# Layer five's VectorE order, and third-round sums and products two blocks at a time, in a DCN-v2 cross network on one core

## The chip, the cores and the metric

One core of one Trainium2 chip runs the whole kernel. The metric is the device time of one execution in microseconds, as a median over runs. Five engines work in parallel and wait for each other on semaphores: TensorE (PE in the profile, with PEld for its weight loads), VectorE (DVE), ScalarE (ACT), GpSimd (POOL) and SyncE (SP, which here issues nearly all DMAs; a queue's own instructions stand as SPq or ACTq).

## The reference

The inputs are `x0` (4096 x 416), six matrices `ws` (416 x 416 each) and six biases `bs`, all bfloat16.

```python
def reference(x0, ws, bs):
    x = x0
    for l in range(ws.shape[0]):
        x = x0 * (x @ ws[l] + bs[l]) + x
    return x
```

## The kernel before, in words

The layers are taken as x(l+1) = x0 * c(l+1), where c gathers 1 plus the sum of all products x @ w + b so far. Layers one to five work on transposed data (features on the 128 partitions, rows of the batch along the free dimension); the sixth layer turns back to rows, so that the result can be written out.

**Tiles.** The batch is cut in two halves of 2048 rows (`s` = 0, 1). The 416 features are three blocks of 128 (`m` = 0, 1, 2) and a remainder of 32, which is packed four groups to a tile. So a layer has six main tiles (s, m), called A, Bt, C (s = 0) and Dt, E, F (s = 1) in layer five, and two remainder tiles. Each main tile is evicted from PSUM in two pieces of 1024 columns (`h` = 0, 1).

**Layer five** is `feeding_layer`, and its VectorE work is written out by hand; `pin` keeps that order on the engine. For each tile ScalarE evicts a piece to a buffer `t` (L332). VectorE adds it to the running sum `CM` (`add`, L340, 128x1024), then multiplies by x0 into `XH`, the input of layer six (`mul`, L344, one 128x2048 operation for most tiles). When a tile's sum is complete and `mul` has read it, `rows_out` adds layer six's bias in place (L348) and SP issues a DMA transpose (`xl_dmat`, L231) that brings the sum to row order in `XLrows`, for the addition in layer six. `rem` and `rem_out` do the same for the remainder (L373, L375, L379), and `xl_rem` copies it on ScalarE to its place in `XLrows` (L311). SP works through its DMAs in the order of the program: the transposes of A, Bt, C, Dt, E and F, and after them all the outputs.

**Layer six** has four rounds of eight blocks of 128 rows. In a round TensorE makes eight products of 128x416 in four two-bank PSUM tiles. ScalarE casts a product from PSUM to a `t` buffer (L505). VectorE adds `XLrows` in place (the sum, L507), then multiplies by `X0rows` into an `o` buffer (the product, L495). SP then issues the output DMA (L496). `pending` delays each product until after the next sum, so that it doesn't stand right behind its own sum. In rounds one and two (layout `PAIRS`) two blocks that lie side by side in one PSUM tile are cast, summed, multiplied and written together. In round three (`TURNS`) the first two blocks go together and the other six singly. In round four (`ENDS`) all eight go singly; TensorE itself adds the row sums of the last three, and the very last block is multiplied straight from PSUM, its output issued by ScalarE's queue.

The buffers that turn over here are six `t` (`tpool`), ten `o` (`opool`) and four PSUM tiles.

Of the kernel before, what the change touches and what calls it, by code (L numbers as in the profile page):

```python
# [10 lines left out]
ALU = mybir.AluOpType  # L11
# [5 lines left out]
def kernel(  # L17
# [7 lines left out]
    nc = tc.nc  # L25
    B, D = x0.shape
# [19 lines left out]
    out_v = out.rearrange("(bt p) d -> p bt d", p=P)  # L46
# [11 lines left out]
    X0rows = big.tile([P, NBT, D], BF16)  # L58
# [11 lines left out]
    def col0(s, g):  # L70
        return SW * s + CW * g
# [8 lines left out]
    def pin(ins):  # L80
        tc.keep_in_program_order(ins)
# [33 lines left out]
    for g in range(1, NG):  # L115
        dst, src = WR[32 * g:32 * g + 32, 0, :], WR[0:R, 0, :]
# [113 lines left out]
    def xl_dmat(s, k):  # L230
        nc.sync.dma_start_transpose(out=XLrows[:, 16 * s:16 * s + 16, 128 * k:128 * k + 128],  # L231
                                    in_=CM[:, k, SW * s:SW * s + SW])
# [73 lines left out]
    def xl_rem(s):  # L306
        dst = XLrows[:, 16 * s:16 * s + 16, NK * P:D].rearrange("p (g i) r -> p i g r", g=NG)
        src = scrR[s][:].rearrange("p i (g r) -> p i g r", g=NG)
        n = 4 if s else 2
        for i in range(0, 4, n):  # L310
            pin(nc.scalar.copy(dst[:, i:i + n], src[:, i:i + n]))  # L311
# [13 lines left out]
    def feeding_layer(l, cur, curR, nxt, nxtR):  # L325
        tiles = [(s, m) for s in range(NS) for m in range(NK)]
        pts, ts = {}, {}

        def evict(t):
            for h in range(2):  # L330
                ts[t + (h,)] = tpool.tile([P, 2 * CW], BF16, name="t")
                nc.scalar.activation(ts[t + (h,)][:], pts[t][h][:].rearrange("p a b -> p (a b)"), ACT.Identity,  # L332
                                     bias=bM[:, t[1], l:l + 1], scale=1.0)

        def c_of(t, h):
            c0 = col0(t[0], 2 * h)
            return CM[:, t[1], c0:c0 + 2 * CW]

        def add(t, h):
            pin(nc.vector.tensor_tensor(out=c_of(t, h), in0=ts[t + (h,)][:], in1=c_of(t, h), op=ALU.add))  # L340

        def mul(t, h=0, n=2):
            c0, w = col0(t[0], 2 * h), n * CW
            pin(nc.vector.tensor_tensor(out=nxt[t[0]][:, t[1], 2 * CW * h:2 * CW * h + w], in0=CM[:, t[1], c0:c0 + w],  # L344
                                        in1=XM0[:, t[1], c0:c0 + w], op=ALU.mult))

        def last_bias(c, bias):
            pin(nc.vector.tensor_scalar(out=c, in0=c, scalar1=bias, scalar2=None, op0=ALU.add))  # L348

        def rows_out(t):  # L350
            s, m = t
            c = CM[:, m, SW * s:SW * s + SW]
            if s:
                c = c.rearrange("p (g r) -> p g r", g=NG)[:, :, 0:CW // 2]
            last_bias(c, bM[:, m, LL:L])
            xl_dmat(s, m)

        A, Bt, C, Dt, E, F = tiles
        layer_products(l, 0, tiles, pts, cur, curR, evict)
        evict(Bt)  # L360
        pr2 = psum.tile([P, 2, CW], FP32, tag="ps", name="pr2")
        for s in range(NS):
            mm_rem(l, s, pr2[:, s, :], cur, curR)
        tr = []
        for s in range(NS):
            tr.append(tpool.tile([P, 2 * CW], BF16, name="t"))
            for a in range(0, CW, CW // 2):
                nc.scalar.activation(tr[s][:, a:a + CW // 2], pr2[:, s, a:a + CW // 2], ACT.Identity, bias=bR[:, l:l + 1], scale=1.0)

        def rem(s, op):  # L370
            part = slice(CW * s, CW * s + CW)
            if op == ALU.add:
                pin(nc.vector.tensor_tensor(out=CR[:, part], in0=tr[s][:, 0:CW], in1=CR[:, part], op=op))  # L373
            else:
                pin(nc.vector.tensor_tensor(out=nxtR[:, part], in0=CR[:, part], in1=XR[0][:, part], op=op))  # L375

        def rem_out(s):
            last_bias(CR[:, CW * s:CW * s + (CW // 2 if s else CW)], bR[:, LL:L])
            nc.sync.dma_start_transpose(out=scrR[s][:], in_=CR[:, CW * s:CW * s + CW])  # L379

        add(A, 0)
        mul(A, 0)
        add(A, 1)
        add(Bt, 0)
        mul(A, 1)
        rows_out(A)
        add(Bt, 1)
        rem(0, ALU.add)
        mul(Bt, 0, 4)
        rem(0, ALU.mult)  # L390
        rem(1, ALU.add)
        rem_out(0)
        rows_out(Bt)
        rem(1, ALU.mult)

        layer_products(l, 2, tiles, pts, cur, curR, evict)
        evict(Dt)
        add(C, 0)
        add(C, 1)
        rem_out(1)  # L400
        mul(C, 0, 4)
        add(Dt, 0)
        rows_out(C)
        add(Dt, 1)
        mul(Dt, 0, 4)

        def before_last(t):
            xl_rem(0)
            evict(t)

        layer_products(l, 4, tiles, pts, cur, curR, before_last)
        evict(F)
        add(E, 0)
        rows_out(Dt)
        add(E, 1)
        mul(E, 0, 4)
        add(F, 0)
        rows_out(E)
        add(F, 1)
        mul(F, 0, 4)  # L420
        rows_out(F)
        xl_rem(1)

    cur, curR = XH[0:2], XR[1]
    for l in range(1, LL):
        nxt, nxtR = [[h for h in XH if h is not cur[0] and h is not cur[1]][0], cur[0]], XR[1 + (l % 2)]
        if l == LL - 1:
            feeding_layer(l, cur, curR, nxt, nxtR)
            cur, curR = nxt, nxtR
            break  # L430
        tiles = [(s, m) for s in range(NS) for m in range(NK)]
        pts = {}

        def finish(t):
            for h in range(2):
                ew_main(l, t[0], t[1], h, pts[t][h], nxt)

        for n in range(0, len(tiles), 2):
            layer_products(l, n, tiles, pts, cur, curR, finish)
            finish(tiles[n + 1])  # L440
            if n == 0:
                rem_pair(l, cur, curR, nxtR)
        cur, curR = nxt, nxtR

    l = LL
# [37 lines left out]
    pending = []  # L483

    def rows(q, g0, n):
        s, i = quads[q]
        b0 = 16 * s + 4 * g0 + i
        return slice(b0, b0 + 4 * (n - 1) + 1, 4)

    def close_product():  # L490
        while pending:
            src, q, g0, n, eng = pending.pop()
            b = rows(q, g0, n)
            o = opool.tile([P, 2, D], BF16, name="o")
            pin(nc.vector.tensor_tensor(out=o[:, 0:n, :], in0=src, in1=X0rows[:, b, :], op=ALU.mult))  # L495
            eng.dma_start(out_v[:, b, :], o[:, 0:n, :])  # L496

    def ew(q, g0, n, src, eng, added, direct):
        if direct:
            close_product()  # L500
            pending.append((src, q, g0, n, eng))
            return
        t = tpool.tile([P, 2 * CW], BF16, name="t")
        tv = t[:, 0:n * D].rearrange("p (a d) -> p a d", a=n)
        nc.scalar.copy(tv, src)  # L505
        if not added:
            pin(nc.vector.tensor_tensor(out=tv, in0=tv, in1=XLrows[:, rows(q, g0, n), :], op=ALU.add))  # L507
        close_product()
        pending.append((tv, q, g0, n, eng))

    PAIRS = [(0, 0), (0, 1), (1, 0), (1, 1), (2, 0), (2, 1), (3, 0), (3, 1)]
    TURNS = [(0, 0), (0, 1), (1, 0), (2, 0), (3, 0), (1, 1), (2, 1), (3, 1)]
    ENDS = [(0, 0), (1, 0), (2, 0), (0, 1), (3, 0), (1, 1), (2, 1), (3, 1)]
    rounds = [(0, PAIRS, 2), (2, PAIRS, 2), (4, TURNS, 2), (6, ENDS, 1)]
    for q, at, done in rounds:
        tiles = [psum.tile([P, 2, CW], FP32, tag="ps", name=f"py{n}") for n in range(4)]
        bank = [tiles[n][:, a, :] for n, a in at]

        final = q + 2 == NQ

        def close(u, n):
            tl, a = at[u]
            ew(q + u // 4, u % 4, n, tiles[tl][:, a:a + n, 0:D], nc.scalar if final and u == 7 else nc.sync,
               final and u >= 5, final and u == 7)

        for u in range(done):
            if q == 0:
                mm_q_open(q, u, bank[u])
            else:
                mm_q_full(q, u, bank[u], False)  # L530
        mm_q_rem(q, bank[0:4], done)
        close(0, done)
        mm_q_rem(q + 1, bank[4:8], 0)
        for u in range(done, 8):
            mm_q_full(q + u // 4, u % 4, bank[u], True, final and u >= 5)
            if at is not PAIRS:
                close(u, 1)
            elif u % 2:
                close(u - 1, 2)
    close_product()  # L540


# [28 lines left out]
```

## Time and profile before

| | us |
|---|---|
| median of 3 runs | 129.75 (129.72 to 129.80) |
| the profiled execution: its own time | 129.89 |
| the profiled execution: span in the trace | 128.1 |
| outside the span | 1.79 |
| PE busy | 122.5 (96% of the span) |
| DVE busy | 102.9 (80%) |
| ACT busy | 87.7 (68%) |

The granted TensorE clock of the profiled execution is 0.997 over the span. The span runs from the first instruction to the last; times below are in us from its start. In a timeline an instruction is given with its start, its duration, engine, line, operation, out<-in with sizes, and a count where neighbours are merged. VectorE's instructions overlap at their ends, so what one of them costs the next is read from start to start, and not from its duration.

### The profile page before, as it was taken

What the parts mean: (1) busy time and instruction counts of PE and PEld (TensorE: products, weight loads), DVE (VectorE), ACT (ScalarE), POOL (GpSimd) and SP (SyncE); (2) the same over time, 40 slices, a digit from 0 to 9 for tenths busy, and PEclk for the clock granted to TensorE, in tenths of its full rate; (3) what the DMA queues carried; (4) which work ended last, traced back from release to release, by engine and by line L of the source; (5) the groups of instructions that cost most, each with busy time, mean ns of one, the idle gap of its engine ahead of it and who ended that gap; (6) DMA issues with size and microseconds to landing.
All of it is one profiled execution on the core that took longest, in us unless ns stands there. A gap on an engine that the chain in (4) does not pass through costs nothing.

```text
span 128.1 us, 3968 instructions
## 1 busy us (share of the span) xinstructions
PE 122.5 (96%) x1684; PEld 55.3 (43%) x1686; DVE 102.9 (80%) x198; ACT 87.7 (68%) x109; POOL 5.6 (4%) x18
## 2 busy tenths in 40 slices
PE   7999999999999999999999999999999999999960
PEld 3343343444445444444444445444444345445530
DVE  0124579774979898989898989898999999999990
ACT  0038867887858667858667858667859697679740
POOL 4004002500000000000000000000000000000000
PEclk9999999999999999999999999999999999999998
DMA  3999999999950000000000000000089999999764
GB/s 99 232 229 223 178 235 263 304 331 335 339 155 0 5 0 0 8 0 5 0 5 0 5 0 5 0 0 5 0 164 91 176 168 213 157 303 292 248 199 142
DMA packets 42230, 16.38 MB, mean 128 GB/s; under 512 B 31034, under 2 KB 42212, under 8 KB 42212
## 3 DMA queue, kind: packets, MB, share of 16 engines
q1 hardware_dynamic: 37432, 15.40, 53.2%
q10 hardware_dynamic: 4780, 0.72, 3.6%
q8 instruction: 13, 0.21, 0.7%
q14 instruction: 5, 0.04, 0.1%
HBM read 6.15 MB, written 3.41 MB: 75 GB/s over the span
## 4 chain that ended last, share of the span: by engine, by line
PE 86%; DMA 4%; DVE 3%; ACTq 2%; issue 1%; ACT 0%; DVEq 0%
PE pt L208 50%; PE ph L240 11%; PE py L463 10%; PE pt L214 5%; PE pr L224 5%; DMA xrig<-in_x_dram 4%; DVE t L507 2%; PE pr L220 2%; PE ph L247 1%; PE py L476 1%; DVE o L495 1%; PE py L457 1%; ACTq L86 1%; ACTq L108 1%; ACT t L505 0%
## 5 line engine op out<-in xcount | busy, mean ns | idle before, releaser
L208 PE MATMUL pt<-XH,WM 128*32 128x512 bf16 x1152 | 65.2, 379 | 0.0
L187 ACT ACTIVATE t<-pt,bM 128x1024 bf16<-128x1024 f32 x36 | 37.2, 1115 | 13.7 <-PE pt L214 13.7
L208 PEld LDWEIGHTS <-WM 128*32 128x32 bf16 x1152 | 29.7, 97 | 33.8 <-issue 5.1
L188 DVE TENSOR_TENSOR CM<-t,CM 128x1024 bf16<-128x1024 bf16 x36 | 24.7, 687 | 4.3 <-ACT t L187 4.3
L189 DVE TENSOR_TENSOR XH<-CM,XM 128x1024 bf16<-128x1024 bf16 x36 | 24.9, 692 | 2.6
L505 ACT CAST t<-py 128x416 bf16<-128x416 f32 (+1 forms) x22 | 14.2, 649 | 4.2 <-PE py L463 1.8
L463 PE MATMUL py<-WM,XH 128*128 128x416 bf16 x90 | 17.0, 339 | 0.0
L240 PE MATMUL ph<-XM,WM 128*128 128x512 bf16 x70 | 16.3, 379 | 0.3 <-DMA XM<-in_x_dram 0.2
L332 ACT ACTIVATE t<-pt,bM 128x1024 bf16<-128x1024 f32 x12 | 12.4, 1115 | 4.1 <-PE pt L214 4.1
L181 ACT ACTIVATE CM<-ph,bM 128x1024 bf16<-128x1024 f32 x12 | 12.5, 1114 | 3.5 <-PE ph L247 3.5
L183 DVE TENSOR_TENSOR XH<-CM,XM 128x512 bf16<-128x512 bf16 x24 | 8.9, 434 | 4.0 <-ACT CM L181 3.9
L463 PEld LDWEIGHTS <-XH 128*128 128x128 bf16 x90 | 8.5, 98 | 7.5 <-issue 1.2
L240 PEld LDWEIGHTS <-WM 128*128 128x128 bf16 x72 | 6.8, 98 | 8.7 <-issue 1.3
L495 DVE TENSOR_TENSOR o<-t,X0rows 128x416 bf16<-128x416 bf16 (+1 forms) x22 | 9.9, 463 | 0.0
L507 DVE TENSOR_TENSOR t<-t,XLrows 128x416 bf16<-128x416 bf16 (+1 forms) x20 | 9.3, 470 | 0.1
L340 DVE TENSOR_TENSOR CM<-t,CM 128x1024 bf16<-128x1024 bf16 x12 | 8.1, 687 | 0.3 <-ACT t L332 0.3
L344 DVE TENSOR_TENSOR XH<-CM,XM 128x2048 bf16<-128x2048 bf16 (+1 forms) x7 | 7.5, 1070 | 0.4
L214 PE MATMUL pt<-XR,WR 32*128 32x512 bf16 x96 | 7.3, 379 | 0.0
L224 PE MATMUL pr<-XH,WM 128*32 128x512 bf16 x96 | 6.6, 379 | 0.0
L196 ACT ACTIVATE t<-pr,bR 128x256 bf16<-128x256 f32 x12 | 4.7, 475 | 1.6 <-PE pr L224 1.6
L114 ACT ACT_TABLE_LOAD x1 | 1.3, 1283 | 6.1 <-DMA XM<-in_x_dram 6.1
L224 PEld LDWEIGHTS <-WM 128*32 128x32 bf16 x120 | 3.2, 97 | 3.2
(61 smaller groups left out, 59.2 us busy)
## 6 DMA issues: line engine op xcount, KB each, us to landing
X0rows<-in_x_dram SPq DMA_DIRECT2D x8, 312.0 KB, 6.7
out_dram<-o SPq DMA_DIRECT2D x9, 208.0 KB, 3.0
WM<-in_ws_dram SPq DMA_DIRECT2D x5, 312.0 KB
out_dram<-o SPq DMA_DIRECT2D x13, 104.0 KB, 1.9
X0rows<-in_x_dram SPq DMA_DIRECT2D x4, 208.0 KB, 6.3
WR<-in_ws_dram SPq DMA_DIRECT2D x4, 130.0 KB, 5.4
WM<-in_ws_dram ACTq DMA_DIRECT2D x1, 312.0 KB
XM<-in_x_dram SPq DMA_TRANSPOSE x8, 5.7
```

The source lines that it names most:

```text
L181: nc.scalar.activation(c, src, ACT.Identity, bias=bias, scale=1.0)
L187: nc.scalar.activation(t[:], src, ACT.Identity, bias=bias, scale=1.0)
L188: nc.vector.tensor_tensor(out=c, in0=t[:], in1=c, op=ALU.add)
L189: nc.vector.tensor_tensor(out=x, in0=c, in1=XM0[:, m, c0:c0 + 2 * CW], op=ALU.mult)
L208: nc.tensor.matmul(pts[g // 2][32 * q:32 * q + 32, g % 2, :], lhsT=WM[:, l, k, 128 * m + 32 * q:128 * m + 32 * q + 32], rhs=cur[s][:, k, C ...
L214: nc.tensor.matmul(pts[g // 2][:, g % 2, :], lhsT=WR[32 * g:32 * g + 32, l, 128 * m:128 * m + 128], rhs=curR[32 * g:32 * g + 32, CW * s:CW ...
L224: nc.tensor.matmul(pr[32 * g:32 * g + 32, :], lhsT=WM[:, l, k, NK * P:D], rhs=cur[s][:, k, CW * g:CW * g + CW], start=False, stop=(k == NK ...
L240: nc.tensor.matmul(pt[:, gl, :], lhsT=WM[:, 0, k, 128 * m:128 * m + 128], rhs=cur[:, k, c0:c0 + CW], start=(k == 0 and not after_row), sto ...
L332: nc.scalar.activation(ts[t + (h,)][:], pts[t][h][:].rearrange("p a b -> p (a b)"), ACT.Identity, bias=bM[:, t[1], l:l + 1], scale=1.0)
L463: nc.tensor.matmul(py[:, 0:D], lhsT=q_x(q, g, k), rhs=WM[:, l, k, :], start=((not closes) and k == 0), stop=(closes and not adds and k == ...
L505: nc.scalar.copy(tv, src)
L507: pin(nc.vector.tensor_tensor(out=tv, in0=tv, in1=XLrows[:, rows(q, g0, n), :], op=ALU.add))
```

## The change

In layer five, `rows_out` of a tile used to stand right behind the `mul` that reads the same sum (A, F), or between the two `add`s of the next tile, so that the second `add` stood right in front of the `mul` that reads it (C and Dt, E and F). Now the second `add` of Bt, Dt and F goes ahead of `rows_out` of A, C and E. `rows_out(F)` leaves `feeding_layer`: it is called in layer six, behind the first sum of round one and ahead of the second.

In round three of layer six, the six single blocks are taken as three pairs. The two of a pair lie in different PSUM tiles, so they are still cast one by one, to one `t` buffer; one sum and one product of 128x832 then take the place of two of each of 128x416. The two output DMAs of such a pair stay single, and both are issued after the common product. Rounds one, two and four keep their groups.

```diff
@@ feeding_layer
         add(A, 1)
         add(Bt, 0)
         mul(A, 1)
+        add(Bt, 1)
         rows_out(A)
-        add(Bt, 1)
         rem(0, ALU.add)
...
         mul(C, 0, 4)
         add(Dt, 0)
+        add(Dt, 1)
         rows_out(C)
-        add(Dt, 1)
         mul(Dt, 0, 4)
...
         mul(E, 0, 4)
         add(F, 0)
+        add(F, 1)
         rows_out(E)
-        add(F, 1)
         mul(F, 0, 4)
-        rows_out(F)
         xl_rem(1)
+        return lambda: rows_out(F)
@@ layer six
     def close_product():
         while pending:
-            src, q, g0, n, eng = pending.pop()
-            b = rows(q, g0, n)
+            src, q, g0, n, parts, eng = pending.pop()
             o = opool.tile([P, 2, D], BF16, name="o")
-            pin(nc.vector.tensor_tensor(out=o[:, 0:n, :], in0=src, in1=X0rows[:, b, :], op=ALU.mult))
-            eng.dma_start(out_v[:, b, :], o[:, 0:n, :])
+            pin(nc.vector.tensor_tensor(out=o[:, 0:n, :], in0=src, in1=X0rows[:, rows(q, g0, n), :], op=ALU.mult))
+            for j in range(0, n, parts):
+                eng.dma_start(out_v[:, rows(q, g0 + j, parts), :], o[:, j:j + parts, :])

-    def ew(q, g0, n, src, eng, added, direct):
+    def ew(q, g0, srcs, eng, added, direct):
...
         t = tpool.tile([P, 2 * CW], BF16, name="t")
+        n = 0
+        for src in srcs:
+            w = src.shape[1]
+            nc.scalar.copy(t[:, n * D:n * D + w * D].rearrange("p (a d) -> p a d", a=w), src)
+            n += w
         tv = t[:, 0:n * D].rearrange("p (a d) -> p a d", a=n)
-        nc.scalar.copy(tv, src)
         if not added:
             pin(nc.vector.tensor_tensor(out=tv, in0=tv, in1=XLrows[:, rows(q, g0, n), :], op=ALU.add))
         close_product()
-        pending.append((tv, q, g0, n, eng))
+        pending.append((tv, q, g0, n, n // len(srcs), eng))
...
-        close(0, done)
+        close([range(done)])
+        if q == 0:
+            last_rows_out()
         mm_q_rem(q + 1, bank[4:8], 0)
         for u in range(done, 8):
             mm_q_full(q + u // 4, u % 4, bank[u], True, final and u >= 5)
-            if at is not PAIRS:
-                close(u, 1)
+            if at is ENDS:
+                close([[u]])
             elif u % 2:
-                close(u - 1, 2)
+                close([[u - 1, u]] if at is PAIRS else [[u - 1], [u]])
     close_product()
```

More of the change, by code (lines that the diff above doesn't have):

```diff
@@ L427 @@
         if l == LL - 1:
-            feeding_layer(l, cur, curR, nxt, nxtR)
+            last_rows_out = feeding_layer(l, cur, curR, nxt, nxtR)
             cur, curR = nxt, nxtR
@@ L491, in close_product @@
         while pending:
-            src, q, g0, n, eng = pending.pop()
-            b = rows(q, g0, n)
+            src, q, g0, n, parts, eng = pending.pop()
             o = opool.tile([P, 2, D], BF16, name="o")
-            pin(nc.vector.tensor_tensor(out=o[:, 0:n, :], in0=src, in1=X0rows[:, b, :], op=ALU.mult))
-            eng.dma_start(out_v[:, b, :], o[:, 0:n, :])
-    def ew(q, g0, n, src, eng, added, direct):
+            pin(nc.vector.tensor_tensor(out=o[:, 0:n, :], in0=src, in1=X0rows[:, rows(q, g0, n), :], op=ALU.mult))
+            for j in range(0, n, parts):
+                eng.dma_start(out_v[:, rows(q, g0 + j, parts), :], o[:, j:j + parts, :])
+    def ew(q, g0, srcs, eng, added, direct):
         if direct:
             close_product()
-            pending.append((src, q, g0, n, eng))
+            pending.append((srcs[0], q, g0, 1, 1, eng))
             return
         t = tpool.tile([P, 2 * CW], BF16, name="t")
+        n = 0
[3 more added lines that the diff above has]
+            n += w
         tv = t[:, 0:n * D].rearrange("p (a d) -> p a d", a=n)
-        nc.scalar.copy(tv, src)
         if not added:
@@ L519, with close @@
         final = q + 2 == NQ
[L521 to L524, printed above, removed]
+        def close(groups):
+            u, direct = groups[0][0], final and groups[0][0] == 7
+            srcs = [tiles[at[g[0]][0]][:, at[g[0]][1]:at[g[0]][1] + len(g), 0:D] for g in groups]
+            ew(q + u // 4, u % 4, srcs, nc.scalar if direct else nc.sync,
+               final and u >= 5, direct)
         for u in range(done):
```

## The prediction

> **What bounds the kernel now.** I read the chain of waits in order of time first. TensorE carries it, matmul behind matmul, from 8 us on. At 119.06 it passes to ScalarE and VectorE, and stays with VectorE until the last product:
>
> ```profile
> 118.77 0.29 PE py L480 x4
> ...
> 119.08 0.52 ACT t L505
> 119.59 0.03 issue
> 119.63 0.38 DVE t L507
> ...
> 124.28 0.79 DVE o L495 x2
> ```
>
> The hand-over at 119.59 is inferred from semaphores. I checked it by counting sums: the cast that ends at 119.59 is block 0 of round four, and its sum is the one at 120.77. So VectorE is over 1 us behind ScalarE there. Its timeline says since when:
>
> ```profile
> 102.07 0.69 DVE L340 TENSOR_TENSOR CM<-t,CM 128x1024 bf16<-128x1024 bf16 x1
> 102.67 0.48 DVE L348 TENSOR_SCALAR CM<-CM,bM 128x1024 bf16<-128x1024 bf16 x1
> ...
> 106.00 0.69 DVE L340 TENSOR_TENSOR CM<-t,CM 128x1024 bf16<-128x1024 bf16 x1
> 106.78 1.23 DVE L344 TENSOR_TENSOR XH<-CM,XM 128x2048 bf16<-128x2048 bf16 x1
> 108.05 0.49 DVE L348 TENSOR_SCALAR CM<-CM,bM 128x1024 bf16<-128x1024 bf16 x1
> 108.59 1.09 DVE L507 TENSOR_TENSOR t<-t,XLrows 128x832 bf16<-128x832 bf16 x2
> ...
> 116.12 0.59 DVE L507 TENSOR_TENSOR t<-t,XLrows 128x832 bf16<-128x832 bf16 x1
> 116.63 0.59 DVE L495 TENSOR_TENSOR o<-t,X0rows 128x832 bf16<-128x832 bf16 x1
> ...
> 117.92 0.37 DVE L507 TENSOR_TENSOR t<-t,XLrows 128x416 bf16<-128x416 bf16 x1
> 118.20 0.37 DVE L495 TENSOR_TENSOR o<-t,X0rows 128x416 bf16<-128x416 bf16 x1
> 118.49 0.37 DVE L507 TENSOR_TENSOR t<-t,XLrows 128x416 bf16<-128x416 bf16 x1
> ...
> 124.48 0.59 DVE L495 TENSOR_TENSOR o<-py,X0rows 128x416 bf16<-128x416 f32 x1
> ```
>
> From 88.3 to 125.1 no line has an idle time in front of it (19.77 of 20.60 us busy from 88 to 108.6, then 16.5 of 16.5), so a gain anywhere there reaches the tail. The price of an operation is its distance to the next start. An `add` costs 0.60 when something unrelated follows (102.07 to 102.67), but 0.78 when the `mul` that reads its result follows (106.00 to 106.78). A 128x416 sum or product costs 0.285, and a 128x832 one 0.50, not twice 0.285.
>
> Last, the floor under VectorE and the way out:
>
> ```profile
> 119.98 2.09 ACT L505 CAST t<-py 128x416 bf16<-128x416 f32 x4 [0.39 <-PE py L463]
> ...
> 122.99 0.51 ACT L505 CAST t<-py 128x416 bf16<-128x416 f32 x1 [0.21 <-PE py L469]
> ...
> 123.74 1.29 SPq L496 DMA_DIRECT2D out_dram<-o  x3
> 124.64 0.88 SPq L496 DMA_DIRECT2D out_dram<-o  x2
> ...
> 125.10 0.40 ACTq L496 DMA_DIRECT2D out_dram<-o  x1
> ```
>
> The last cast ends at 123.50 and TensorE at 123.67, while the last product starts at 124.48. SP's last output is issued at 125.12, though its product ended at 124.57, because SP spends 0.43 to 0.48 on each. It lands last, at 127.21; ScalarE's, issued at 125.11, lands at 127.02. After 127.21 there are only fixed closing steps.
>
> **Layer five, part by part.** Nothing is added or removed; only distances change.
> - `mul(A, 1)` to `rows_out(A)` was 0.72 (90.94 to 91.66). With `add(Bt, 1)` between, the distance is that of 102.07 to 102.67, 0.60: gain 0.12. `add(Bt, 1)` would start at 91.54, and its eviction ended at 91.30, so it is free to move. But `add(C, 1)`, at 96.93 before, would come to 96.81, and the eviction it reads ends at 96.86: 0.07 goes back, 0.05 is left.
> - `add(Dt, 1)` to `mul(Dt)` was 0.78 (100.14 to 100.92), now 0.60: 0.18. Its eviction ends at 98.87, its new start is 99.42.
> - `add(F, 1)` to `mul(F)`: the 0.78 shown, now 0.60: 0.18. Its eviction ends at 104.70, its new start is 105.37.
> - `mul(F)` to `rows_out(F)` was 1.27. `mul(E)`, with an unrelated `add` behind it, took 1.14 (103.86 to 105.00): 0.13.
> - `rows_out(F)` to the first sum was 0.54, `rows_out(E)` to the next `add` 0.40. The sum doesn't read what `rows_out` writes, so I can't say where the 0.14 is from: between 0 and 0.14. I take half, since one row speaks for each end.
>
> Sum: 0.05 + 0.18 + 0.18 + 0.13 + 0.07 = 0.61, bounds 0.54 to 0.68. The other `add`-`mul` neighbours (E, A's first half) stay as they are.
>
> **What waits on the moved steps.** Each `rows_out` has a transpose on SP behind it, 1.75 to 3.27 us of SP's time. A's starts at 92.9 instead of 92.45 and ends at 94.7; the next on SP waits for VectorE until 95.4, so it is covered by 0.7. C's `rows_out` ends at 100.8 instead of 100.2, while SP is busy with the remainder until 101.0: covered by 0.2. E's is not covered: SP is free at 105.94 and now gets E at 106.45 instead of 106.11. Then F goes out at 109.3 instead of 108.93 (its `rows_out` ends near 108.5, so it is E's transpose that it waits for) and lands near 114.1 instead of 113.75; its reader is the first sum of round three, at 115.5: 1.4 us of room. The outputs are queued behind F. The first goes out near 112.6 instead of 112.29, and the products that are ready by then go one behind the other, as they did before until 115.24. Until the ten `o` buffers come round, near 119, nobody waits for that. The first sum needs C's transpose, which landed at 105.89; its new start is 107.5. I cost all of this at nothing.
>
> A page of the Trainium skill speaks against this part: "VectorE: DVE Perf Modes", section "The DRAIN you can't avoid", has the next operation start only when the pipe is empty, and a semaphore between neighbours cost nothing more; by it a new order gains nothing. The rows above, 0.60 and 0.78 for the same `add`, don't agree with that.
>
> **Round three.** Twelve operations at 0.285 (3.42) become six at 0.50 (3.01): gain 0.41. The second cast of a pair has to end before the pair's sum; how that works out is in the walk below.
>
> **What the tail can take.** VectorE offers 0.61 + 0.41 = 1.02, but it then runs up against the casts, which TensorE paces. I walk it with the casts' old ends plus 0.03. The first sum of round three would start at 115.51 (cast ends 115.40). The pairs' sums: 116.5, 117.5, 118.53 (second casts end 116.39, 117.45, 118.50; the last ended at 118.60 only because it waited for a `t` buffer that VectorE held, which it needn't now). Round four: the sum of block 0 waits for its cast (119.59) and starts at 119.62, 1.15 earlier than before; the pair's product goes at 119.91. The sum of block 1 waits for its cast (120.49): 120.52, against 121.34, so 0.82. From there the old distances hold to the product of block 5 at 123.09. Block 6 waits for the cast that ends at 123.50: 123.54, against 124.19. The last product starts at 123.83, against 124.48: gain 0.65. Since ScalarE stands in the way from 119.6 on, a gain in layer five of only 0.5 would end the same.
>
> SP: from the second pair's product, ended at 119.6, eleven outputs queue for it. At 0.45 apiece, and waiting for a product now and then, the last is issued at 124.28, against 125.12: 0.84. ScalarE's is issued at 124.46, against 125.11: 0.65. Whichever of the two lands later ends the kernel, after 1.9 to 2.1 us: between 0.65 and 0.85 earlier. I take the middle, 0.75: span 128.10 - 0.75 = 127.35, its own time 129.89 - 0.75 = 129.14. The profiled execution was 0.14 above the median of the runs, so the median goes from 129.75 to 129.00. The likeliest case alone spans 128.85 to 129.15.
>
> **The rivals.** A measurement of this kernel tells 0.2% (0.26 us) from no change.
> - *The order in layer five gains nothing*: the 0.18 could move to another neighbour. Then only round three's 0.41 is left, no cast holds VectorE up, and the last product starts at 124.07: 129.34. Against it: the eight `add`s of layer five with something unrelated behind them cost 0.60 or 0.61, the four with their reader behind them 0.78 to 0.80. It is also what the Trainium skill's rule gives.
> - *The output DMAs are the bound*: in the last 4 us the DMA engines move some 130 rows of 832 bytes per half microsecond. If that were their limit, outputs that start 0.3 later at 112.6 couldn't end earlier: 129.75. Against it: between 114 and 118 the same queue moved 180 to 200 per half microsecond.
> - *Slower: SP's issue of pairs.* Each pair gives SP two outputs at once, and the last eleven form one queue from 119.63. If one costs x, the last is issued at 119.63 + 10x, which is later than 125.12 from x = 0.55 on. The outputs of 128x832 did cost 0.49 to 0.65 between 112.29 and 115.24; at 0.60 the last is issued at 125.63, 0.5 later: 130.25. Against it: single blocks show 0.43 to 0.48 when queued. This also decides if all the rest comes true.
>
> **How the numbers follow.** The forecast has 0.74, layer five without a gain 0.08, the DMA bound 0.06, SP's queue 0.12. So faster 0.82, same 0.06, slower 0.12. The range goes from 128.75 (0.85 gained, and 0.15 for outputs that land with less between them) to 129.75, where it takes in the first two rivals and leaves SP's out.
>
> **What would show it.** In the changed profile: start to start 0.60 behind `add(Dt, 1)` and `add(F, 1)`, and 1.14 behind `mul(F)`; the first sum near 107.5; three sums and products of 128x832 in round three, 0.50 apart; idle time in front of the sums of blocks 0 and 1 of round four, ended by ScalarE; the last product near 123.8 and ScalarE's output issue near 124.5. I am wrong if VectorE still has no idle time in round four, if SP's last issue comes over 0.4 after ScalarE's, or if a sum of round three waits for a DMA.

## The result and the profile after

The changed kernel takes 129.47 us (median of 20 runs, 129.29 to 130.26) against 129.76 (20 runs): a ratio of 0.9977, 95% interval 0.9969 to 0.9984. That is 0.3 us faster, where 0.75 was forecast. The profiled execution took 129.42 us, with a span of 127.52 (128.10 before). That execution of before was 0.13 above its median and this one 0.05 below, so 0.18 of the 0.47 between the two profiles is the choice of executions.

In the chain of waits, in order of time, TensorE now keeps the lead until 122.88, and VectorE's long tail is gone:

```profile
122.85 0.03 PE py L469
122.88 0.02 issue
122.91 0.52 ACT t L507
123.42 0.02 issue
123.44 0.06 DVE o L494
```

VectorE's timeline of the changed kernel (start, duration, operation), from the end of layer five to the last product:

```profile
104.67 1.28 DVE L340 TENSOR_TENSOR CM<-t,CM 128x1024 bf16<-128x1024 bf16 x2
105.88 0.48 DVE L348 TENSOR_SCALAR CM<-CM,bM 128x1024 bf16<-128x1024 bf16 x1
106.28 1.22 DVE L344 TENSOR_TENSOR XH<-CM,XM 128x2048 bf16<-128x2048 bf16 x1
107.41 0.58 DVE L511 TENSOR_TENSOR t<-t,XLrows 128x832 bf16<-128x832 bf16 x1
107.91 0.48 DVE L348 TENSOR_SCALAR CM<-CM,bM 128x1024 bf16<-128x1024 bf16 x1
108.31 0.58 DVE L511 TENSOR_TENSOR t<-t,XLrows 128x832 bf16<-128x832 bf16 x1
...
116.36 0.58 DVE L511 TENSOR_TENSOR t<-t,XLrows 128x832 bf16<-128x832 bf16 x1
...
119.53 0.38 DVE L511 TENSOR_TENSOR t<-t,XLrows 128x416 bf16<-128x416 bf16 x1
119.83 0.58 DVE L494 TENSOR_TENSOR o<-t,X0rows 128x832 bf16<-128x832 bf16 x1
120.43 0.38 DVE L511 TENSOR_TENSOR t<-t,XLrows 128x416 bf16<-128x416 bf16 x1
...
123.73 0.58 DVE L494 TENSOR_TENSOR o<-py,X0rows 128x416 bf16<-128x416 f32 x1
```

Two `add`s of F take 1.21 from the first start to `rows_out(E)`, `mul(F)` is followed after 1.13, and the last product starts 0.75 earlier by the trace's own clock. So VectorE did what was forecast. It now runs right behind the casts: block 0's ends at 119.50 and its sum starts at 119.53, block 1's at 120.40 and 120.43. It has next to no idle time there (4.71 of the 4.80 us from 119.50 to 124.30 are busy), less than the prediction's signs had it, because the product of 128x832 in front still fills the gap. The outputs did not follow. In the timeline of the two queues that issue them (start, duration, queue, line):

```profile
120.92 0.45 SPq L496 DMA_DIRECT2D out_dram<-o  x1
121.86 0.33 SPq L496 DMA_DIRECT2D out_dram<-o  x1
...
124.74 0.39 SPq L496 DMA_DIRECT2D out_dram<-o  x1
...
124.35 0.38 ACTq L496 DMA_DIRECT2D out_dram<-o  x1
```

ScalarE's last output went out 0.75 earlier than before, but SP's last only 0.38 (124.74, before 125.12), although its product had ended at 123.82. SP's is 0.39 behind ScalarE's, just inside the 0.4 that the prediction gave as a sign against it. SP's landed at 126.63, ScalarE's at 126.31. Between 121.37 and 121.86 SP stood still, although the product it was to send had ended at 121.09. The queue of the kernel before shows such a stop too, between 121.22 and 121.75, but there the product to be sent ended only at 121.43:

```profile
120.89 0.33 SPq L496 DMA_DIRECT2D out_dram<-o  x1
121.75 0.33 SPq L496 DMA_DIRECT2D out_dram<-o  x1
```

The starts of the traces differ by up to 0.4 us against TensorE's work, so the tails are compared from the start of the last matmul of each. These are traces of one execution each:

| kernel | last matmul starts | last product | ScalarE's last issue | SP's last issue | last landing | from there to the end | ratio to before (95%) |
|---|---|---|---|---|---|---|---|
| before | 123.49 | +0.98 | +1.61 | +1.63 | +3.72 | 0.89 | 1 |
| changed | 123.41 | +0.32 | +0.94 | +1.33 | +3.22 | 0.90 | 0.9977 (0.9969 to 0.9984) |
| order alone | 123.46 | +0.33 | +0.94 | +1.17 | +3.07 | 0.89 | 0.9957 (0.9945 to 0.9970) |
| pairs alone | 123.45 | +0.57 | +1.18 | +1.94 | +3.73 | 0.90 | 1.0014 (1.0001 to 1.0026) |
| changed, one DMA per pair | 123.45 | +0.33 | +0.94 | +1.03 | +3.04 | 1.09 | 0.9967 (0.9955 to 0.9979) |
| changed, two outputs on ScalarE | 123.58 | +0.32 | +0.94 | +0.90 | +3.26 | 1.02 | 0.9976 (0.9965 to 0.9987) |
| both of these | 123.51 | +0.33 | +0.94 | +0.55 | +2.90 | 1.20 | 0.9961 (0.9948 to 0.9973) |
| changed, four DMAs per pair | 123.33 | +0.33 | +3.27 | +6.23 | +8.00 | 0.97 | 1.0344 (1.0330 to 1.0358) |
| one DMA per pair, 4 spare loads | 123.45 | +0.33 | +0.94 | +0.83 | +2.90 | 0.94 | 0.9947 (0.9935 to 0.9960) |
| order alone, 4 spare loads | 123.36 | +0.33 | +0.94 | +1.10 | +3.06 | 1.07 | 0.9968 (0.9957 to 0.9980) |
| order, singles, one DMA for two | 123.22 | +0.33 | +0.94 | +1.17 | +3.09 | 1.09 | 0.9972 (0.9961 to 0.9984) |
| the same, 4 spare loads | 123.41 | +0.33 | +0.94 | +1.04 | +3.02 | 0.83 | 0.9951 (0.9939 to 0.9964) |
| one DMA per pair, 8 spare loads | 123.44 | +0.33 | +0.94 | +0.81 | +2.88 | 1.03 | 0.9957 (0.9943 to 0.9970) |

The column of the last product has one value, 0.32 or 0.33, wherever layer five has the new order. What differs between those kernels is SP's last issue, and the time from the last landing to the end. The prediction called these closing steps fixed. Between before and the changed kernel they are (0.89 and 0.90), but over all traces they take 0.83 to 1.20 us. SP ends with five waits for the landings, in a fixed order and about 0.065 us apart. When the output that lands last belongs to the first of these waits, the other four still follow (1.09); when it belongs to the fourth, only one does (0.89). With two outputs on ScalarE's queue 0.15 to 0.2 comes on top.

### The profile page after: what moved, and what is told of

Same layout as the page of the kernel before. It is cut to its first block, busy times and chain, and to the rows that moved or that the text cites. A ratio compares the mean times of both kernels' runs of the same rounds, so it can differ in the third digit from the quotient of the medians.

```text
span 127.5 us, 3953 instructions
## 1 busy us (share of the span) xinstructions
PE 122.6 (96%) x1684; PEld 55.3 (43%) x1686; DVE 102.4 (80%) x192; ACT 87.7 (69%) x109; POOL 5.1 (4%) x18
## 4 chain that ended last, share of the span: by engine, by line
PE 90%; DMA 4%; ACTq 2%; DVEq 1%; issue 0%; ACT 0%; DVE 0%
PE pt L208 50%; PE py L463 12%; PE ph L240 11%; PE pt L214 5%; PE pr L224 5%; DMA xrig<-in_x_dram 4%; PE pr L220 2%; PE py L476 2%; PE ph L247 2%; PE py L457 1%; ACTq L86 1%; DVEq L573 1%; ACTq L108 1%; ACT t L507 0%; PE tpr L163 0%
## 5 line engine op out<-in xcount | busy, mean ns | idle before, releaser
L494 DVE TENSOR_TENSOR o<-t,X0rows 128x832 bf16<-128x832 bf16 (+1 forms) x19 | 9.4, 504 | 0.1
L511 DVE TENSOR_TENSOR t<-t,XLrows 128x832 bf16<-128x832 bf16 (+1 forms) x17 | 8.9, 521 | 0.0
```

## The experiments

**One half of the change at a time.** The theory was that SP's output queue sets the end of the changed kernel, and that the pairs fill it in bursts. Rival A was that the DMA engines set it, rival B that ScalarE's last output does. The first kernel has the new order of layer five with round three as before:

```diff
 layer five as changed, layer six as before, and:
-            feeding_layer(l, cur, curR, nxt, nxtR)
+            last_rows_out = feeding_layer(l, cur, curR, nxt, nxtR)
...
         close(0, done)
+        if q == 0:
+            last_rows_out()
```

> Layer five's new order alone; round three as before, with six single sums, products and outputs. Theory (SP's output queue, which the pairs fill in bursts, sets the end of the changed kernel): without the bursts SP follows the products, VectorE's 0.6 us arrive almost whole, last product near 123.9, SP's last issue near 124.6; 129.3, ratio to before 0.9965. Rival A (the DMA engines or the landing itself set the end, whatever SP does): no gain, 0.999 to 1.000. Rival B (ScalarE's last output sets it, SP is hidden): 0.6 us, 0.9955.

It came out at 0.9957 (0.9945 to 0.9970), 0.55 us. The order alone is not slower than the whole change, and by the ratios it is 0.26 us faster, though the intervals touch; in the traces its last landing is 0.15 earlier. Its timelines, VectorE's and the two queues':

```profile
123.79 0.58 DVE L495 TENSOR_TENSOR o<-py,X0rows 128x416 bf16<-128x416 f32 x1
...
120.32 0.38 SPq L496 DMA_DIRECT2D out_dram<-o  x1
121.23 0.33 SPq L496 DMA_DIRECT2D out_dram<-o  x1
...
124.63 0.40 SPq L496 DMA_DIRECT2D out_dram<-o  x1
...
124.40 0.38 ACTq L496 DMA_DIRECT2D out_dram<-o  x1
```

The last product stands where it stands in the changed kernel: the order alone brings VectorE to the casts. SP is still last, 0.23 behind ScalarE, and stops once here too (120.70 to 121.23).

The second kernel has the pairs alone, with the `add`s and `rows_out`s of before:

```diff
 layer six as changed, layer five as before, and:
         close([range(done)])
-        if q == 0:
-            last_rows_out()
```

> Round three by pairs alone; layer five as before. Theory: VectorE gains 0.41 and the last product starts near 124.1, but SP gets its eleven last outputs in bursts from 120.2 on, at 0.48 each and with one stall, so that its last issue stays at 125.1 to 125.4: ratio 0.999 to 1.002. Rival A: 0.999 to 1.000. Rival B: 0.4 us, 0.997.

It is 1.0014 (1.0001 to 1.0026): no gain, and rather a small loss, as the theory had it. VectorE's gain is there and SP throws it away (VectorE's timeline, then the queues'):

```profile
124.02 0.58 DVE L494 TENSOR_TENSOR o<-py,X0rows 128x416 bf16<-128x416 f32 x1
...
125.39 0.41 SPq L496 DMA_DIRECT2D out_dram<-o  x1
...
124.63 0.38 ACTq L496 DMA_DIRECT2D out_dram<-o  x1
```

The last product starts 0.42 earlier against TensorE, which is the 0.41 of the sum, and SP's last issue comes 0.31 later. Rival B is out: ScalarE's last issue came 0.43 earlier against TensorE and the time did not fall.

**Relieving SP.** Here each pair of the changed kernel goes out in one DMA:

```diff
-        pending.append((tv, q, g0, n, n // len(srcs), eng))
+        pending.append((tv, q, g0, n, n, eng))
```

> The whole change, but each pair of round three goes out in one DMA of 128x2x416 in place of two of 128x416: three issues less on SP, the same bytes, VectorE's work unchanged. Theory: SP's last issue comes from 124.74 to near 124.3 and the end with it, until ScalarE's output (issued at 124.35) is last: 0.2 to 0.4 us under the changed kernel, ratio to before 0.995 to 0.996. Rivals A and B: as the changed kernel, 0.9977.

The ratio is 0.9967 (0.9955 to 0.9979), 0.13 us under the changed kernel where 0.2 to 0.4 was expected: the direction is right, the size is a miss, and the interval holds the changed kernel's 0.9977 too. SP's last issue came forward by 0.30 against TensorE for three issues less, which should have saved over 1 us of SP's time; the stop had moved to where nothing hid it (121.73 + 0.35 to 122.60). The last landing came 0.18 earlier, and the closing waits took 0.19 longer.

Or block 6's output goes to ScalarE's queue:

```diff
-        ew(q + u // 4, u % 4, srcs, nc.scalar if direct else nc.sync,
+        ew(q + u // 4, u % 4, srcs, nc.scalar if final and u >= 6 else nc.sync,
```

> The whole change, but the last output but one (block 6 of round four) is issued by ScalarE's queue, which is idle after its last cast, in place of SP's. Theory: it goes out near 123.9 and not at 124.74, SP's last is now that of block 5 at 124.25, the very last block still at 124.35: 0.2 to 0.4 us under the changed kernel, ratio 0.995 to 0.996. Rival A: 0.9977. Rival B: 0.9977, or more if the two outputs on one queue hold each other up.

0.9976 (0.9965 to 0.9987): nothing. SP's last issue did come 0.43 earlier against TensorE, so SP was relieved. But ScalarE's two issues now fell next to SP's last two:

```profile
124.02 0.88 ACTq L496 DMA_DIRECT2D out_dram<-o  x2
```

The last two landed 2.2 and 2.3 us after their issue (126.66 and 126.83), against 1.9 and 2.0 in the changed kernel. So four outputs issued within 0.55 us seem to hold each other up, and rival A to have a share in the last 0.3 us; this rests on one trace. The Trainium skill says in "DMA: Bandwidth & Descriptors", "Rules for kernel authors", that spreading DMAs over several issuing engines saves issue time only, since they run on the same DMA engines. These landings agree.

Both edits together, on the changed kernel:

> One DMA per pair and block 6's output on ScalarE's queue, both on top of the whole change. If SP's queue is all that binds: SP's last issue (block 5) near 124.0, ScalarE's near 123.9 and 124.4, the last landing 0.2 to 0.3 us before that of the kernel with one DMA per pair alone, ratio 0.9945 to 0.9955. If outputs issued close together on two queues hold each other up, as the kernel with two outputs on ScalarE suggests (landings 2.2 and 2.3 us after issue, not 1.9): 0.9965 to 0.9975.

0.9961 (0.9948 to 0.9973), between the two expectations. Its last landing (+2.90) is as early as that of the best kernel, but its closing steps are the longest, 1.20; so it tells little beyond one DMA per pair alone.

**The dose.** If SP's issues are the price, more of them must cost more. Each output of a pair was cut in two halves of 64 partitions:

```diff
+                for h in ([slice(0, 64), slice(64, P)] if parts < n else [slice(0, P)]):
+                    eng.dma_start(out_v[h, rows(q, g0 + j, parts), :], o[h, j:j + parts, :])
```

> Dose of the suspected cost: each of the two outputs of a pair in round three is cut in two DMAs of 64 partitions, so SP issues six more in that round; bytes and VectorE's work as in the whole change. If SP's queue sets the end: 6 times 0.35 to 0.48 later, 2.1 to 2.9 us over the changed kernel, ratio 1.014 to 1.02. If SP is hidden: 0.9977.

1.0344 (1.0330 to 1.0358), 4.5 us slower, with the same bytes to move and VectorE's last product unmoved (+0.33). SP sets the end, and by more than expected: the starts of the halves lie 0.52 to 0.72 apart (mostly 0.60 to 0.64), where whole blocks lie 0.39 to 0.50 apart when queued. My 0.35 to 0.48 apiece was taken from whole blocks; twelve halves at 0.62 in place of six blocks at 0.45 would be 4.7 us, and the time rose by 4.8 over the changed kernel. ScalarE's output went out 2.3 us later as well, though its product was ready; why is not shown.

**SP's stop.** In the traces that had been taken by then, SP stands still once between the 28th and the 29th instruction of the output phase, counting the waits that stand as instructions of their own, whichever output that is: the last block of round three in the kernel before, block 0 of round four in the changed one, block 2 with one DMA per pair. In the kernel with one DMA per pair, four loads of 0.8 KB that nobody reads were put behind SP's loads, to shift the count:

```diff
+    for g in range(NG):
+        nc.sync.dma_start(spare[32 * g:32 * g + 1, :], bs[LL:LL + 1, :])
```

> One DMA per pair, and four spare loads of 0.8 KB (a bias row nobody reads) at the end of SP's loads, eight SP instructions more than with one DMA per pair. In all six traces so far SP stands still for 0.5 us once, between its 28th and 29th instruction of the output phase, whichever output that is. If that goes by the count of instructions, it now comes before the 21st, where SP waits for VectorE anyway: last SP issue near 124.2 instead of 124.5, 0.2 to 0.3 us under the kernel with one DMA per pair, ratio 0.994 to 0.995. If the stop goes by the clock, by the output or by the DMAs under way: it stays before the output of block 2 of round four, ratio 0.9967.

0.9947 (0.9935 to 0.9960), the best ratio of the series. The stop moved, by two outputs and not by the four that I had expected: each spare load is one instruction, without a wait of its own, so they are four and not eight. It now stands before block 0 of round four (timeline of SP's and ScalarE's queues):

```profile
120.48 0.37 SPq L499 DMA_DIRECT2D out_dram<-o  x1
121.38 0.35 SPq L499 DMA_DIRECT2D out_dram<-o  x1
...
124.28 0.41 SPq L499 DMA_DIRECT2D out_dram<-o  x1
...
124.40 0.38 ACTq L499 DMA_DIRECT2D out_dram<-o  x1
```

That product ended at 121.14, so less than half of the stop costs anything, and SP's last issue is ahead of ScalarE's, with a single output on ScalarE's queue.

The same four loads on the kernel with the order alone:

> Layer five's order alone, with the same four spare loads. If the stop goes by the count of instructions, it comes four outputs earlier, near 118.8; singles leave SP little room behind it, so that its last issue moves from 124.63 to 124.3 or 124.4: 0.1 to 0.3 us under the order alone, ratio 0.9935 to 0.995. If it doesn't: 0.9957.

0.9968 (0.9957 to 0.9980): a miss. The stop moved by two outputs here too (119.20 + 0.39 to 120.11), but SP's last issue is at +1.10 against +1.17. With singles, VectorE gives SP an output every 0.57 and SP needs nearly 0.5, so from 119 on there is no room that could swallow the stop, wherever it is. The last landing is at +3.06 against +3.07, and the closing steps are 0.18 longer here, so no gain could come of it.

**Are VectorE's pairs worth anything?** Singles on VectorE, but two neighbours in one output DMA:

```diff
+            half = g0 % 2 if n == 1 and 4 <= q < 6 else None
...
+            elif half == 1:
+                eng.dma_start(out_v[:, rows(q, g0 - 1, 2), :], held[0][:])
```

> Layer five's order, round three with single sums and products as in the kernel before, but the outputs of two neighbours share a buffer and go out in one DMA behind the second product. SP issues as often as with one DMA per pair; VectorE has six operations more than there. Theory (the order alone takes VectorE to the floor that the casts set, and only SP's issues count): as the pairs with one DMA, 0.996 to 0.997. Rival (VectorE's pairs bring their 0.41 once SP is relieved): 0.3 to 0.4 us slower than those, 0.999 to 1.000.

And with the four spare loads:

> The same with four spare loads on SP, so that SP's stop comes two outputs earlier (before the output of block 0 of round four). Theory: as the pairs with one DMA and four spare loads, 0.9945 to 0.996. Rival (VectorE's pairs bring something): 0.998 or more.

0.9972 (0.9961 to 0.9984) and 0.9951 (0.9939 to 0.9964), beside 0.9967 and 0.9947 with VectorE's pairs: the same within the intervals, and the last product at +0.33 and +0.32 as everywhere. With layer five in its new order, the pairs on VectorE bring nothing that these runs can tell.

Last, eight spare loads with VectorE's pairs and one DMA for each (the edit against the kernel with four):

```diff
-    for g in range(NG):
-        nc.sync.dma_start(spare[32 * g:32 * g + 1, :], bs[LL:LL + 1, :])
+    for g in range(2 * NG):
+        nc.sync.dma_start(spare[16 * g:16 * g + 1, :], bs[LL:LL + 1, :])
```

> Pairs with one DMA and eight spare loads: SP's stop should come before the second pair's output (its 11th), where SP waits 0.7 us for VectorE in any case and the stop costs nothing. Last SP issue near 124.2, before ScalarE's at 124.4, which is then the last to go out: up to 0.1 us under the kernel with four spare loads, 0.994 to 0.995. If the stop doesn't move on by the count of instructions: 0.9947 to 0.9967, with the stop in another place.

0.9957 (0.9943 to 0.9970), within the interval of the kernel with four, but not the 0.994 to 0.995 that was expected. The stop went where expected, before the second pair's output, where SP waits for a product that ends at 119.57:

```profile
118.55 0.37 SPq L499 DMA_DIRECT2D out_dram<-o  x1
119.60 0.38 SPq L499 DMA_DIRECT2D out_dram<-o  x1
```

SP then follows the products to 122.86; its last three outputs queue again, but ScalarE's output lands last (126.32, SP's 126.01). In this trace the last product sets the last landing, and an earlier issue on SP would not move it.

## Why the prediction was right or wrong

- **VectorE in layer five: right, and 0.03 over its bounds.** From layer five's first `add` to the second sum of round one, the time fell by 0.71 (88.32 to 109.10 before, 88.24 to 108.31 after); the sum was 0.61 with bounds 0.54 to 0.68. The open 0.14 in front of the first sum went entirely: `mul(F)` to that sum is 1.13, `rows_out(F)` to the next 0.40. The Trainium skill's rule on the pipe's emptying ("VectorE: DVE Perf Modes", "The DRAIN you can't avoid"), read as in the prediction, would let a new order gain nothing; the same section says that an operation that is not held starts earlier. This kernel shows 0.55 us for the order alone.
- **The transposes behind the moved steps: covered, as costed.** F's landed at 113.85, and the sums of round three never waited for it.
- **Round three on VectorE: right in size, worth nothing.** Alone it moved the last product by 0.42. But I added 0.41 to 0.61 and let the walk absorb the surplus, without asking which of the two was the surplus. Layer five's part brings the last product to within 0.01 of the floor by itself.
- **What the tail can take: right for VectorE, to 0.02** (sums of blocks 0 and 1 forecast at 119.62 and 120.52, found at 119.53 and 120.43 in a trace that runs 0.08 early; last product 0.66 earlier against TensorE).
- **SP: the step that failed.** "The last is issued at 124.28, against 125.12: 0.84" should have read 124.7 to 124.8, 0.3 to 0.4. Two things were left out. The stop of half a microsecond stands in the trace of before as well, between 121.22 and 121.75, where SP waited for its product anyway until 121.43 and could catch up by 123.2; in the changed kernel it falls into a queue without gaps. And behind it SP's outputs came 0.48 apart on average (0.44 to 0.50), not 0.45. The rival "SP's issue of pairs" named the mechanism and priced its point at 0.55 per output. From 119.57 to 124.74 it was 0.517 with the stop: below that point, so not slower, but enough to take most of SP's share.
- **The size.** "Whichever of the two lands later" was right as a rule: SP's 1.33 sets +3.22. Of the 0.75, the trace shows 0.50 against TensorE: SP's queue took 0.25. The runs show 0.29; the choice of executions explains 0.18 of that second difference. The 129.47 lies within the range of 128.75 to 129.75 only because the range was drawn wide for two rivals that did not come; the likeliest case alone, 128.85 to 129.15, was missed.

So by the ratios the gain of 0.29 consists of about 0.55 for the order, less about 0.26 for the pairs; the traces show 0.15 of this at the last landing, behind SP's later issue. The pairs cost in both settings, 0.18 us alone and 0.26 on top of the order, though each interval by itself reaches almost to nothing.

What the stop is stays open. That it goes by SP's count of instructions is shown (it moved by two outputs with four spare instructions and by four with eight; an output is two instructions, its wait and its DMA): in all 13 traces it stands right in front of the 80th instruction that the trace has for SP. The traces have one more hint. Among the DMA queues that the profile lists is "q14 instruction", and in all 13 traces a single packet of 8 KB on it starts 1.08 to 1.49 us behind the stop's beginning and moves with the stop (at 122.81 in the changed kernel, 122.28 with four spare loads, 120.41 with eight). So the stop may have to do with how SP is supplied with its program. No run here shows that it is the cause.

## What to carry to other kernels

Ask of each of two gains what it brings once the other is in: where the next engine's floor is near, the second is surplus, and its side effects are all that remains of it. A larger operation ahead of a queue hands its results over later and in bursts, so follow the last stage (here the issuing of outputs, 0.48 us each) to the end with the same care as the engine that is changed, gaps and stops of the old trace included. One DMA for the two blocks of a pair, and the stop moved to where SP waits anyway, made the best version here, 0.9947 (0.9935 to 0.9960); but layer five's order alone, at 0.9957 (0.9945 to 0.9970), can't be told from it.

## What the runs showed of the hardware that was not expected

SP stood still for 0.44 to 0.47 us at a fixed count of its own instructions, in every kernel, and a packet on the queue "q14 instruction" followed each time. Half an output (64 partitions) cost SP 0.52 to 0.72 us between starts, mostly 0.6, more than a whole one (0.39 to 0.50). Of four outputs issued from two queues within 0.55 us the last two landed 2.2 to 2.3 us after issue, against 1.9 to 2.0. From the last landing to the end of the span it took 0.83 to 1.20 us, by the place of the last output in SP's closing waits.
